# Three changes to the schedule of a fused attention and channel-mix kernel: norm matmuls later and in another PSUM bank, squares in pairs, and one square behind a product

## The chip, the cores and the metric

One core of one Trainium2 chip. The time is that of one execution on the device, in microseconds (us); every figure quoted as a time is the median of several runs. A run's page comes from one profiled execution. The engines are TensorE (PE, with PEld for its weight loads), VectorE (DVE), ScalarE (ACT) and GpSimd (POOL).

Some executions have a mean granted TensorE clock of 0.989 to 0.996 in place of 0.998 to 1.000, and most of these are 1 to 3 us longer (the kernel before: 517.25 at 1.000 and 520.41 at 0.989).

The traces show where the lower clock costs. In profiles at 0.994 to 0.996 the granted clock is 0.83 from 20 to 30 us and 1.00 in the other stretches up to 505 us, and the first matmul of the down projection starts at 52.5 to 53.0 us. So a length measured from that matmul on compares kernels without the clock's disturbance; I call it the length after the head.

## The reference

```python
# attention over channels: q, k, v are [4, 6208, 256]
qn = q / (norm(q, axis=1) + 1e-6);  kn = k / (norm(k, axis=1) + 1e-6)   # norms over the 6208 tokens
s  = kn.transpose(0, 2, 1) @ qn / tau          # 256 x 256 for each batch
a  = softmax(s);   x = v @ a
# channel mix
xk = mu_k * x + (1 - mu_k) * x_prev;   xr likewise with mu_r   # x_prev: the token before
k  = relu(xk @ w_k)                            # 1024 features
out = sigmoid(xr @ w_r) * ((k * k) @ w_v)
```

## The kernel before

The first batch's covariance and softmax make up the first 40 us or so (the head). After that the kernel is a pipeline over blocks of 512 tokens (48 of them, and one of leftovers), with eight steps to a block. In each step TensorE does an up projection for block i+1 (128 features), a part of the down projection for block i, now and then the gate, x of block i+2, and a piece of the covariance of the *next* batch. ScalarE does the relu, the evictions and the squares of q and k; VectorE squares the relu, mixes, and sums the squares. Every instruction's place in the program's order is fixed by hand.

The relu and its square, one 128-feature row at a time:

```python
kr = p2.tile([P, M], BF16, name="kr", tag="kr", bufs=4)
nc.scalar.activation(kr[:, :m], kT_ps[:, :m], AF.Relu, scale=RH)
...
nc.vector.tensor_tensor(st[i, "kk"][:, fh, :m], kr[:, :m], kr[:, :m], op=OP.mult)
```

The norm of one group of 512 tokens: VectorE sums the squares into `t1`, TensorE sums over the partitions by a one-column matmul, ScalarE copies the result out of PSUM. The program places the pool `ps`, into which this kernel's matmuls write, in PSUM; in it the tags `g` (gate) and `xT` (x) own one buffer each, called a bank here, and the norm used the gate's:

```python
n_ps = ps.tile([P, 4], F32, name="n_ps", tag="g")
for i in range(2):
    for h in range(2):
        nc.tensor.matmul(n_ps[:, 2*i+h : 2*i+h+1], t1[:rows, i, h*P:(h+1)*P], ones_b[:rows], ...)
nc.scalar.copy(ssq[b][:, :, g], n_ps)
```

The loop's order, cut to what matters (i is the block, j the step):

```python
if j in (2, 6): gate_act(i, j // 4)            # ScalarE empties the gate's bank
up(i + 1, j)                                   # matmuls, relu
if j > 0: square(i + 1, j - 1)                 # VectorE
...
if j in (0, 1, 4, 5): gate_mm(i, ...)          # fills the gate's bank
down(i, j)
if j in (0, 2): x_half(n, j // 2)              # n = i + 2; fills and empties the bank of x
if j == 4: mix_delta(n)
if j in (5, 6): mix(n, "xk", j - 5)            # VectorE; the next block's up projection needs it
...
elif j in (3, 7) or j in (2, 6) and len(norms) > 1: take_norm()
```

Of the kernel before, what the change touches and what calls it, by code (L numbers as in the profile page):

```python
# [10 lines left out]
F32 = mybir.dt.float32  # L11
BF16 = mybir.dt.bfloat16
AX = mybir.AxisListType.X
AF = mybir.ActivationFunctionType
OP = mybir.AluOpType
# [3 lines left out]
def kernel(  # L19
# [13 lines left out]
    nc = tc.nc  # L33
# [3 lines left out]
    P = 128  # L37
    M = 512
    S = M // P
    assert C == 256 and DF == 1024  # L40
    NB = N // M
# [5 lines left out]
    RH = 0.5 ** 0.5  # L47
# [5 lines left out]
    p2 = ctx.enter_context(tc.tile_pool(name="p2", bufs=3))  # L53
    ps = ctx.enter_context(tc.tile_pool(name="ps", bufs=1, space=bass.MemoryType.PSUM))
# [125 lines left out]
    def broadcast(w, tag, **kw):  # L180
        bc_ps = ps.tile([P, 2, P], F32, name="bc_ps", tag=tag, **kw)
        for h in range(2):
            for u in range(3):
                nc.tensor.matmul(bc_ps[:, h], w[:, u, h:h + 1].to_broadcast([P, P]), ident,
                                 start=h == 0 and u == 0, stop=u == 2, skip_group_check=True)
        return bc_ps.rearrange("p h d -> p (h d)")
# [28 lines left out]
    NBLK = len(blocks)  # L215
# [3 lines left out]
    st = {}  # L219
# [99 lines left out]
    def mix(i, key, dh):  # L319
        mu = mu_k_t if key == "xk" else mu_r_t  # L320
        o = st[i, key]
        if i < LAST:
            c = blocks[i][1] * M
            nc.vector.scalar_tensor_tensor(o[:, dh], st[i, "d"][:, dh], mu[:, dh:dh + 1],  # L324
                                           X[:, dh, c:c + M], op0=OP.mult, op1=OP.add)
        else:
            def r(a):
                return a.rearrange("p (b l) -> p b l", b=B)
            nc.vector.scalar_tensor_tensor(r(o[:, dh, :B * L]), r(st[i, "d"][:, dh, :B * L]), mu[:, dh:dh + 1],
                                           xl[:, dh, :, :L], op0=OP.mult, op1=OP.add)  # L330

    def up(i, fh):
        m = size(i)
        if fh == 0:
            st[i, "kk"] = p2.tile([P, 8, M], BF16, name="kk", tag="kk", bufs=2)
        xk = st[i, "xk"]
        kT_ps = ps.tile([P, M], F32, name="kT_ps", tag="kT", bufs=3)
        for dh in range(2):
            nc.tensor.matmul(kT_ps[:, :m], w_k_sb[:, dh, fh * P:(fh + 1) * P], xk[:, dh, :m],  # L339
                             start=dh == 0, stop=dh == 1)  # L340
        kr = p2.tile([P, M], BF16, name="kr", tag="kr", bufs=4)
        nc.scalar.activation(kr[:, :m], kT_ps[:, :m], AF.Relu, scale=RH)  # L342
        st[i, "kr", fh] = kr

    def square(i, fh):
        m = size(i)
        kr = st.pop((i, "kr", fh))
        nc.vector.tensor_tensor(st[i, "kk"][:, fh, :m], kr[:, :m], kr[:, :m], op=OP.mult)  # L348

    def gate_mm(i, s):  # L350
        if s * P >= size(i):
# [87 lines left out]
    norms = []  # L439

    def take_sum():
        if not sums:
            return
        b, g, w = sums.pop(0)
        rows, n = rows_of(g)
        G = groups[b, g]
        if w == 1:
            nc.vector.tensor_tensor(G["sq", 0], G["sq", 0], G["sq", 1], op=OP.add)  # L448
            return
        t1 = pq.tile([P, 2, C], BF16, name="t1", tag="t1", bufs=4)  # L450
        if w == 2:
            nc.vector.tensor_tensor(t1, G["sq", 0][:, 0], G["sq", 0][:, 1], op=OP.add)
        else:
            nc.vector.tensor_copy(t1[:rows], G["sq", 0][:rows, 0])
        norms.append((b, g, t1))

    def take_norm():
        if not norms:
            return
        b, g, t1 = norms.pop(0)  # L460
        rows, n = rows_of(g)
        n_ps = ps.tile([P, 4], F32, name="n_ps", tag="g")
        for i in range(2):
            for h in range(2):
                nc.tensor.matmul(n_ps[:, 2 * i + h:2 * i + h + 1], t1[:rows, i, h * P:(h + 1) * P], ones_b[:rows],
                                 start=i == 0 and h == 0, stop=True, skip_group_check=True)
        nc.scalar.copy(ssq[b][:, :, g], n_ps)  # L467
        if g == GORD[-1]:
            chain.extend(softmax_pieces(b))
# [8 lines left out]
    def softmax_pieces(b):  # L478
        t_sb, e_sb, sm, mx = soft_tiles()
        hold = {}  # L480

        def a():
            hold["n"] = root(ssq[b], 4)

        def a2():
            hold["r"] = inverse(hold["n"], 4)
            if inv_tau != 1.0:
                nc.vector.tensor_scalar_mul(hold["r"][:, 2:], hold["r"][:, 2:], inv_tau)

        def b1():  # L490
            hold["dq"] = spread(hold["r"])

        def bcast():
            hold["bc"] = pn.tile([P, C], F32, name="rq_bc", bufs=1)
            nc.scalar.copy(hold["bc"], broadcast(hold["dq"], "g"))

        def c():
            nc.vector.tensor_tensor(t_sb, s_sb[b], hold["bc"].unsqueeze(1).to_broadcast([P, 2, C]), op=OP.mult)

        def e():  # L500
            for ih in range(2):
                soft_half(b, ih, t_sb, hold["r"][:, 2:], e_sb, sm, mx)

        def f():
            for ih in range(2):
                soft_scale(b, ih, e_sb, sm)

        return [a, None, a2, b1, None, bcast, None, c, e, f]


# [73 lines left out]
    chain = []  # L584
    lst = {}

    for i in range(-2, NBLK):
        for j in range(8):
            T = i * 8 + j
            if i == LAST - 1 and j == 7:  # L590

                st[LAST, "res"] = pq.tile([P, S, D], F32, name="res", tag="f4", bufs=NF)
                for s in range(2):
                    gate_mm(LAST, s)
                gate_act(LAST, 0)
            if j in (2, 6):
                gate_act(i, j // 4)
            if 0 <= i + 1 < NBLK:
                up(i + 1, j)
            if j == 0 and i >= 0:  # L600
                square(i, 7)
            if j > 0 and 0 <= i + 1 < NBLK:
                square(i + 1, j - 1)
            if j == 5:
                finish(i, 0)
            if j == 1:
                finish(i - 1, 1)
            if i >= 0:
                if j in (0, 1, 4, 5) and i < LAST:
                    gate_mm(i, j // 4 * 2 + j % 4)  # L610
                down(i, j)
            n = i + 2
            if n == 0 and j == 0:
                x_first()
            if 0 < n < LAST:
                if j == 0:
                    x_half(n, 0)
                if j == 2:
                    x_half(n, 1)
            if n < NBLK:  # L620

                d = 4 if n != 1 else 3
                if j == d:
                    mix_delta(n)
                if j in (d + 1, d + 2) and n > 0:
                    mix(n, "xk", j - d - 1)
            if j in (0, 1) and 0 <= i + 1 < NBLK:
                mix(i + 1, "xr", j)
            if j == 7 and 2 <= i + 3 < NPE:
                v_transpose_pe(i + 3, st.pop((i + 3, "v")), 0, S, "s")  # L630
            if j == 1 and NPE <= i + 5 < LAST:
                v_transpose_dma(i + 5)
            if j == 2 and NPE < i + 7 < LAST:
                v_load(i + 7)
            bank_g = False
            if chain and (chain[0] is None or chain[0].__name__ != "bcast" or j in (3, 7)):
                f = chain.pop(0)
                if f is not None:
                    f()
                    bank_g = f.__name__ == "bcast"  # L640
            if bank_g:
                pass
            elif j in (3, 7) or j in (2, 6) and len(norms) > 1:
                take_norm()
            if j in (2, 3, 6, 7) or len(sums) > 2:
                take_sum()
            for u in due.get(T, []):
                b, g, s = units[u]
                at = (b - 1) * (NB + 1) + GORD.index(g)
                more_rows(at + 4)  # L650
                unit(b, g, s)
                if g == GORD[-1] and s == S - 1:
                    evac_s(b)
            if i >= 0 and i // NB < B:
                bl = i // NB
                if i % NB == 2 and j == 1:
                    lst["v"] = left_load(bl)
                if i % NB == 4 and j == 3:
                    lst["t"] = left_transpose(lst["v"])
                if i % NB == 6 and j == 4:  # L660
                    left_x(bl, lst["t"])
# [35 lines left out]
```

## Time and profile before

| | before |
|---|---|
| time, three runs | 517.29 us (517.14 to 517.46) |
| span in the profile | 515.3 us |
| TensorE busy / idle | 492.3 / 23 us, of which 12.5 idle in the first 60 us |
| VectorE busy | 451.3 us |
| ScalarE busy | 435.7 us |

The busy share of an average says little here: read the kernel as a head that is fed by DMA (VectorE's casts wait 11.8 us for the loads of q and 3.6 us for those of k), a long middle (60 to 505 us) in which TensorE is meant never to stop, and a short tail. In the middle, the question is only where TensorE's next matmul started later than the one before it allowed. I call the lateness a hole. (In the waits below, `ssq` is the copied norm, `t` the sum of squares, `v_ps` the down projection and `res` its gated product.) The lines of the profile follow in the prediction.

### The profile page before, as it was taken

Reading aid. Unit: us, or ns where it says so; the run is one execution under the profiler, and the core shown is the slowest. Engines: PE = TensorE matmul, PEld = TensorE weight load, DVE = VectorE, ACT = ScalarE, POOL = GpSimd, SP = SyncE. Lnnn points to the kernel's source line nnn. Section 1 sums busy time; section 2 is a strip of 40 time slices with the busy share of each in tenths; the row PEclk is TensorE's granted clock in tenths of the full one; section 3 lists DMA queues with packets and bytes.
Section 4 is the critical chain, followed back from the end, with each engine's and each line's share of the span. In section 5 each row is a group of like instructions: output and inputs, shape, how many; then the busy total and the mean of one; then the engine's idle time right before and its main releaser. Section 6 shows DMA issues by size and latency. Waiting matters only on the chain. (4 is left out here: it accounts for less than half of the span.)

```text
span 515.3 us, 10233 instructions
## 1 busy us (share of the span) xinstructions
PE 492.3 (96%) x3723; PEld 340.5 (66%) x3786; DVE 451.3 (88%) x899; ACT 435.7 (85%) x832; POOL 104.5 (20%) x145
## 2 busy tenths in 40 slices
PE   4699999999999999999999999999999999999996
PEld 2474676767667677677666767667666666666675
DVE  3468899999999999999999999999989888888884
ACT  5778999999989898899999899899787877777773
POOL 0047523332431231221251132100031000000000
PEclk9999999999999999999999999999999999999999
DMA  8999999999999999599699999962298673332113
GB/s 313 396 321 188 181 201 207 194 201 186 186 186 207 164 170 174 115 173 155 109 185 216 167 178 165 142 129 71 62 170 141 122 126 95 94 88 76 58 67 102
DMA packets 143202, 83.51 MB, mean 162 GB/s; under 512 B 51184, under 2 KB 139824, under 8 KB 143152
## 3 DMA queue, kind: packets, MB, share of 16 engines
q0 software_dynamic: 65808, 33.01, 50.1%
q1 hardware_dynamic: 77184, 49.72, 39.5%
q8 instruction: 29, 0.48, 0.4%
q14 instruction: 21, 0.17, 0.1%
q10 hardware_dynamic: 160, 0.13, 0.1%
HBM read 78.71 MB, written 25.43 MB: 202 GB/s over the span
## 5 line engine op out<-in xcount | busy, mean ns | idle before, releaser
L342 ACT ACTIVATE kr<-kT_ps 128x512 bf16<-128x512 f32 (+1 forms) x392 | 232.5, 595 | 37.0 <-PE kT_ps L339 29.8
L387 PE MATMUL v_ps<-w_v_sb,kk 128*128 128x256 bf16 x1536 | 230.4, 273 | 0.5
L339 PE MATMUL kT_ps<-xk,w_k_sb 128*128 128x512 bf16 (+1 forms) x725 | 218.9, 377 | 3.0 <-DVE xk L324 1.3
L348 DVE TENSOR_TENSOR kk<-kr 128x512 bf16<-128x512 bf16 (+1 forms) x392 | 161.7, 417 | 35.1 <-ACT kr L342 31.4
L387 PEld LDWEIGHTS <-kk 128*128 128x128 bf16 x1536 | 150.2, 98 | 57.6
L430 ACT ACTIVATE sq<-qk 128x512 f32<-128x512 bf16 (+1 forms) x147 | 93.2, 634 | 0.0
L339 PEld LDWEIGHTS <-w_k_sb 128*128 128x128 bf16 x784 | 74.8, 98 | 22.0 <-issue 1.0
L358 PE MATMUL g_ps<-w_r_sb,xr 128*128 128x256 bf16 x388 | 73.9, 272 | 2.5 <-ACT ssq L467 1.3
L260 ACT CAST X<-xT_ps 128x512 bf16<-128x512 f32 x94 | 55.5, 590 | 20.0 <-PE xT_ps L258 19.3
L324 DVE SCALAR_TENSOR_TENSOR xr<-delta,mu_r_t,X 128x512 bf16<-128x512 bf16 x96 | 71.5, 745 | 0.0
L358 PEld LDWEIGHTS <-xr 128*128 128x128 bf16 x388 | 37.8, 98 | 49.0 <-issue 5.9
L324 DVE SCALAR_TENSOR_TENSOR xk<-delta,mu_k_t,X 128x512 bf16<-128x512 bf16 x94 | 70.1, 745 | 0.0
L400 DVE SCALAR_TENSOR_TENSOR res<-res,v_ps 128x512 f32<-128x512 f32 x96 | 65.3, 680 | 0.0
L416 POOL DMA_DIRECT2D qk<-in_q_dram x39 | 28.6, 734 | 164.8 <-ACT sq L430 136.7
L393 ACT ACTIVATE res<-g_ps 128x512 f32<-128x512 f32 x97 | 57.8, 596 | 0.4 <-PE g_ps L358 0.4
L258 PE MATMUL xT_ps<-vT,a_sb 128*128 128x512 bf16 x188 | 55.9, 379 | 0.2 <-ACT X L285 0.2
L426 PE MATMUL s_ps<-qk 128*128 128x256 bf16 (+1 forms) x294 | 56.1, 272 | 0.0
L227 POOL DMA_DIRECT2D v_bf<-in_v_dram x48 | 37.3, 781 | 52.4 <-DMA vT<-v_bf 47.4
L448 DVE TENSOR_TENSOR sq<-sq 128x1024 f32<-128x1024 f32 x36 | 43.9, 1219 | 1.0 <-ACT sq L430 1.0
L426 PEld LDWEIGHTS <-qk 128*128 128x128 bf16 (+1 forms) x294 | 26.6, 97 | 12.1 <-issue 1.3
L313 DVE TENSOR_TENSOR delta<-X 128x1024 bf16<-128x1024 bf16 x48 | 32.9, 686 | 0.1
L416 POOL DMA_DIRECT2D qk<-in_k_dram x39 | 28.9, 741 | 6.8 <-DMA qk<-in_q_dram 2.1
(73 smaller groups left out, 235.1 us busy)
## 6 DMA issues: line engine op xcount, KB each, us to landing
out_dram<-res SPq DMA_DIRECT2D x48, 512.0 KB, 3.3
v_bf<-in_v_dram POOLq DMA_DIRECT2D x48, 256.0 KB, 8.1
qk<-in_q_dram POOLq DMA_DIRECT2D x36, 256.0 KB, 8.5
qk<-in_k_dram POOLq DMA_DIRECT2D x36, 256.0 KB, 9.5
f<-in_q_dram SPq DMA_DIRECT2D x12, 512.0 KB, 8.3
f<-in_k_dram SPq DMA_DIRECT2D x11, 512.0 KB, 9.1
vT<-v_bf SPq DMA_TRANSPOSE x44, 6.7
w_k_sb<-in_moe_w_k_dram POOLq DMA_DIRECT2D x1, 512.0 KB, 6.3
```

Source lines behind the costliest of these rows:

```text
L258: nc.tensor.matmul(xT_ps, a_sb[:, b, ih, dh * P:(dh + 1) * P], vT[:, :, ih, :], start=ih == 0, stop=ih == 1)
L324: nc.vector.scalar_tensor_tensor(o[:, dh], st[i, "d"][:, dh], mu[:, dh:dh + 1], X[:, dh, c:c + M], op0=OP.mult, op1=OP.add)
L339: nc.tensor.matmul(kT_ps[:, :m], w_k_sb[:, dh, fh * P:(fh + 1) * P], xk[:, dh, :m], start=dh == 0, stop=dh == 1)
L342: nc.scalar.activation(kr[:, :m], kT_ps[:, :m], AF.Relu, scale=RH)
L348: nc.vector.tensor_tensor(st[i, "kk"][:, fh, :m], kr[:, :m], kr[:, :m], op=OP.mult)
L358: nc.tensor.matmul(g_ps[:, s % 2], xr[:, dh, s * P:(s + 1) * P], w_r_sb[:, dh, :], start=s % 2 == 0 and dh == 0, stop=dh == 1, skip_group_ ...
L387: nc.tensor.matmul(v_ps[:, s % 2], kk[:, fh, s * P:(s + 1) * P], w_v_sb[:, fh, :], start=s % 2 == 0 and fh == 0, stop=fh == 7, skip_group_ ...
L393: nc.scalar.activation(st[i, "res"][:, 2 * u:2 * u + 2], st.pop((i, "g", u)), AF.Tanh, scale=0.5)
L400: nc.vector.scalar_tensor_tensor(r, r, 1.0, st.pop((i, "v", u)), op0=OP.add, op1=OP.mult)
L416: nc.gpsimd.dma_start(qk[:rows, :n, i], src_rows(t, b, g))
L426: nc.tensor.matmul(cov[b][:, ih, :], qk[:rows, s, 1, ih * P:(ih + 1) * P], qk[:rows, s, 0, :], start=g == GORD[0] and s == 0 and ih == 0, ...
L430: nc.scalar.activation(G["sq", s // 2][:rows, s % 2], qk[:rows, s], AF.Square)
```

## The change

The intent: give TensorE nothing to wait for in the middle. Three things are done. (1) The norm's matmuls (and the spread of r, which happens three times in the run) go to the bank of x, at steps 4 and 6, and not before two steps after their sum. (2) The relu rows are squared two at a time. (3) The square that belongs to step 6 is issued behind the mix of xk.

```diff
-        kr = p2.tile([P, M], BF16, name="kr", tag="kr", bufs=4)
-        nc.scalar.activation(kr[:, :m], kT_ps[:, :m], AF.Relu, scale=RH)
+        if fh % 2 == 0:
+            st[i, "kr", fh // 2] = p2.tile([P, 2, M], BF16, name="kr", tag="kr", bufs=3)
+        nc.scalar.activation(st[i, "kr", fh // 2][:, fh % 2, :m], kT_ps[:, :m], AF.Relu, scale=RH)
 ...
-        nc.vector.tensor_tensor(st[i, "kk"][:, fh, :m], kr[:, :m], kr[:, :m], op=OP.mult)
+        if fh % 2 == 0:
+            return
+        nc.vector.tensor_tensor(st[i, "kk"][:, fh - 1:fh + 1, :m], kr[:, :, :m], kr[:, :, :m], op=OP.mult)
 ...
-        norms.append((b, g, t1))
+        norms.append((b, g, t1, T + 2))          # T counts steps; taken only from then on
 ...
-        n_ps = ps.tile([P, 4], F32, name="n_ps", tag="g")
+        n_ps = ps.tile([P, 4], F32, name="n_ps", tag="xT")
 ...                                              # and the spread of r: "g" -> "xT"
-            if j > 0 and 0 <= i + 1 < NBLK:
+            if j > 0 and j != 6 and 0 <= i + 1 < NBLK:
                 square(i + 1, j - 1)
 ...  (mix of xk at steps 5 and 6)
+            if j == 6 and 0 <= i + 1 < NBLK:
+                square(i + 1, j - 1)
 ...
-            elif j in (3, 7) or j in (2, 6) and len(norms) > 1:
+            if j in (4, 6) and not bank_x or j in (3, 5) and len(norms) > 1:
                 take_norm()
```

More of the change, by code (lines that the diff above doesn't have):

```diff
@@ L340, in up @@
                              start=dh == 0, stop=dh == 1)
-        kr = p2.tile([P, M], BF16, name="kr", tag="kr", bufs=4)
-        nc.scalar.activation(kr[:, :m], kT_ps[:, :m], AF.Relu, scale=RH)
-        st[i, "kr", fh] = kr
+        if fh % 2 == 0:
+            st[i, "kr", fh // 2] = p2.tile([P, 2, M], BF16, name="kr", tag="kr", bufs=3)
+        nc.scalar.activation(st[i, "kr", fh // 2][:, fh % 2, :m], kT_ps[:, :m], AF.Relu, scale=RH)
     def square(i, fh):
         m = size(i)
-        kr = st.pop((i, "kr", fh))
-        nc.vector.tensor_tensor(st[i, "kk"][:, fh, :m], kr[:, :m], kr[:, :m], op=OP.mult)
+        if fh % 2 == 0:
+            return
+        kr = st.pop((i, "kr", fh // 2))
+        nc.vector.tensor_tensor(st[i, "kk"][:, fh - 1:fh + 1, :m], kr[:, :, :m], kr[:, :, :m], op=OP.mult)
     def gate_mm(i, s):
@@ L454, in take_sum @@
             nc.vector.tensor_copy(t1[:rows], G["sq", 0][:rows, 0])
-        norms.append((b, g, t1))
+        norms.append((b, g, t1, T + 2))
     def take_norm():
-        if not norms:
+        if not norms or norms[0][3] > T:
             return
-        b, g, t1 = norms.pop(0)
+        b, g, t1, _ = norms.pop(0)
         rows, n = rows_of(g)
-        n_ps = ps.tile([P, 4], F32, name="n_ps", tag="g")
+        n_ps = ps.tile([P, 4], F32, name="n_ps", tag="xT")
         for i in range(2):
@@ L494, in bcast @@
             hold["bc"] = pn.tile([P, C], F32, name="rq_bc", bufs=1)
-            nc.scalar.copy(hold["bc"], broadcast(hold["dq"], "g"))
+            nc.scalar.copy(hold["bc"], broadcast(hold["dq"], "xT"))
         def c():
@@ L634 @@
                 v_load(i + 7)
-            bank_g = False
-            if chain and (chain[0] is None or chain[0].__name__ != "bcast" or j in (3, 7)):
+            bank_x = i >= 0 and i % NB == 6 and j == 4
+            if chain and (chain[0] is None or chain[0].__name__ != "bcast" or j in (4, 6)):
                 f = chain.pop(0)
@@ L639 @@
                     f()
-                    bank_g = f.__name__ == "bcast"
-            if bank_g:
-                pass
-            elif j in (3, 7) or j in (2, 6) and len(norms) > 1:
+                    bank_x = f.__name__ == "bcast"
+            if j in (4, 6) and not bank_x or j in (3, 5) and len(norms) > 1:
                 take_norm()
```

## The prediction

> **What bounds the kernel now.** I read the busy table of the page first, then the busy time by stretches, then the timeline of one block of 512 tokens, then the waits of TensorE, and last the timeline around each of those waits. The page's first part:
>
> ```profile
> PE 492.3 (96%) x3723; PEld 340.5 (66%) x3786; DVE 451.3 (88%) x899; ACT 435.7 (85%) x832; POOL 104.5 (20%) x145
> ```
>
> TensorE looks full and VectorE is close behind. By stretches of 100 us:
>
> ```profile
> 100.00:200.00 100.00, 98.27 (x738) 68.61 (x750) 96.07 (x187) 91.22 (x188) 28.15 (x38) 1.00 1.21 185
> 200.00:300.00 100.00, 98.79 (x736) 69.19 (x749) 95.86 (x188) 91.08 (x183) 25.04 (x35) 1.00 1.00 162
> 300.00:400.00 100.00, 98.30 (x717) 68.14 (x727) 93.19 (x186) 85.90 (x168) 14.60 (x20) 1.00 0.78 130
> 400.00:500.00 100.00, 99.37 (x686) 67.77 (x696) 84.27 (x176) 77.35 (x139) 1.49 (x2) 1.00 0.39 93
> ```
>
> The columns after the length are busy us of PE, PEld, DVE, ACT and POOL. In the first three stretches DVE is 93 to 96% busy, and in the fourth, when the covariance work (squares, sums, norms) has run out, it drops to 84%. PE gains only about one point from that. So DVE is nearly full, but it does not set the pace. The clock column is 1.00 throughout.
>
> A busy PE may still have holes, because the end of a matmul is modelled, so I looked at starts instead. From one block:
>
> ```profile
> 250.56 0.59 PE L339 MATMUL kT_ps<-xk,w_k_sb 128*128 128x512 bf16 x2
> 251.00 0.38 PE L358 MATMUL g_ps<-w_r_sb,xr 128*128 128x256 bf16 x2
> 251.22 0.71 PE L387 MATMUL v_ps<-w_v_sb,kk 128*128 128x256 bf16 x5
> 251.76 0.38 PE L426 MATMUL s_ps<-qk 128*128 128x256 bf16 x2
> 251.98 0.59 PE L339 MATMUL kT_ps<-xk,w_k_sb 128*128 128x512 bf16 x2
> ```
>
> Two 512-column matmuls occupy 251.00-250.56 = 0.44 us, 0.22 each; five of 256 columns occupy 0.54, 0.11 each; two take 0.22. Each group starts when the one before it has streamed. In a block without a stall nothing remains to be won on PE, whatever the other engines do. The gain of this change can only come from the holes. TensorE's waits over the whole run, apart from the head:
>
> ```profile
> PE g_ps L358 <- ACT ssq L467: 1.3, 4, 0.5
> PE kT_ps L339 <- DVE xk L324: 1.3, 3, 0.6
> PE n_ps L465 <- DVE t L452: 0.5, 1, 0.5
> ```
>
> These are idle times after a modelled end; measured start against due start, each hole is longer. One of the first kind:
>
> ```profile
> 269.20 0.24 PE L465 MATMUL n_ps<-ones_b,t 128*128 128x1 bf16 x4
> 269.52 0.59 PE L339 MATMUL kT_ps<-xk,w_k_sb 128*128 128x512 bf16 x2
> 269.90 0.58 ACT L342 ACTIVATE kr<-kT_ps 128x512 bf16<-128x512 f32 x1
> 270.38 0.16 ACT L467 COPY ssq<-n_ps 128x4 f32<-128x4 f32 x1
> 270.59 0.38 PE L358 MATMUL g_ps<-w_r_sb,xr 128*128 128x256 bf16 x2 [0.47 <-ACT ssq L467]
> ```
>
> The norm's four one-column matmuls wrote the gate's PSUM bank at 269.20. ScalarE was behind with the exponentials of the softmax and copied the result out only at 270.38. The gate's next matmul needs the same bank; due at 269.52+2*0.22 = 269.95, it started at 270.59, a loss of 0.63. One of the second kind:
>
> ```profile
> 389.20 0.39 PE L339 MATMUL kT_ps<-xk,w_k_sb 128*128 128x512 bf16 x1
> 389.40 0.75 DVE L324 SCALAR_TENSOR_TENSOR xk<-delta,mu_k_t,X 128x512 bf16<-128x512 bf16 x1
> 390.20 0.38 PE L339 MATMUL kT_ps<-xk,w_k_sb 128*128 128x512 bf16 x1 [0.60 <-DVE xk L324]
> ```
>
> VectorE had done the softmax's last scaling just before and was behind, so the second half of xk came late: due at 389.42, started at 390.20, a loss of 0.78.
>
> [...]
>
> ```profile
> L348 DVE TENSOR_TENSOR kk<-kr 128x512 bf16<-128x512 bf16 x384 | 159.3, 420 | 32.7 <-ACT kr L342 29.1
> L313 DVE TENSOR_TENSOR delta<-X 128x1024 bf16<-128x1024 bf16 x48 | 32.9, 686 | 0.1
> ```
>
> Same operation class and type: 420 ns for 512 columns, 686 for 1024. The slope is 266/512 = 0.52 ns per column and the fixed part 420-266 = 154 ns.
>
> **The change part by part.**
>
> Squares in pairs: 384 instructions of 420 ns (161.3 us of work) become 192 of 1024 columns, taken at 686 ns (131.7 us). That frees 29.6 us of VectorE, 0.62 per block of some 9.9 us. Its share of busy time in the full stretches should fall from 96 to about 90%. None of it lies on TensorE's path in a normal block. It counts only where VectorE is late. The relu's count and cost on ScalarE do not change. The buffers grow from 4 rows to 3 pairs; a relu now needs the square of three pairs back, which is a slot earlier than before, so no new wait there. The square of the pair (4, 5) also moves behind the mix of xk in its slot, which puts xk, what TensorE waited for, first.
>
> What the pairs cost is latency: rows 6 and 7 of a block are now squared together at the block's start. Row 7's square in the block at 250 ran from 250.10 to 250.53, and its matmul was the fifth of the group at 251.22, so at 251.65. A pair would end some 0.27 later, and row 6 is wanted one matmul earlier (251.54): slack of 0.74 in place of 1.12. It holds in a normal block.
>
> Norms in the bank of x: the same matmuls and the same copies, elsewhere. The gate's bank no longer holds a norm, so its wait goes. The bank of x has one buffer too; x is written at steps 0 and 2 of a block, and the norm now comes at 4 or 6 (3 or 5 if two are queued). The copy has two steps of some 1.2 us before the next x at step 0, and x's own eviction ends before step 4. In the bank of the gate it had one step. The spread of r moves likewise, three times in the run.
>
> Two steps behind the sums: the norm's matmul no longer follows its sum at one step's distance, so the wait for t (once, due 114.77, started 115.45: 0.68) goes.
>
> The sum, from starts against due starts in TensorE's timeline. Gate's bank: 270.59 (0.63), 152.90 (0.63), 79.60 (0.34), 63.64 (0.28), 57.73 (0.31), together 2.19. Late VectorE: 115.45 (0.68), 390.20 (0.78), 371.45 (0.59), 51.48 (0.38), together 2.43. All of it is 4.62 us. I take 80%, 3.7, as removed: the early ones are partly the pipeline filling. The tail loses: the last block's final pair (512 columns, 420 ns) stands where a 256-column square (289) stood, and the last gated product queues behind it on VectorE: +0.15, rounded up from 0.13. New waits in other places, a guess: +0.35. Net -3.2 us: 517.3-3.2 = 514.1.
>
> **The rivals.**
>
> 1. VectorE is the real bound, so its 29.6 us come off the time: 488. For it: 96% busy, and 31 us of VectorE's waits are for relus, a loop through three engines. Against it: matmul starts are at their streaming distance in normal blocks, and at 84% VectorE (400 to 500 us) PE gains one point. I give it about 1%.
>
> 2. The bank of x becomes the new single-buffer wait. x's matmuls would wait for the copy of a norm, or a norm for x's eviction; for it, ScalarE was over 1 us late when the exponentials ran, and x's matmul was already followed closely by its eviction. About 39 norms, a tenth of them hit for 0.5 us: +2, so 516. Against it: two steps of slack.
>
> 3. Pairing starves the down projection: row 6 or 7 late at step 1, 0.2 us in each of 48 blocks, +10 us: 523 or so with the gains counted. Against it: the slack of 0.74, and a VectorE with less to do, not more.
>
> 4. Nothing at all: holes reappear because something else is late (ScalarE at 91%, in the softmax stretch); 517.
>
> **Range and chances.** The ceiling is 4.6 us plus some tenths of holes that I did not count, so 512.4 is the low end. The high end takes half the gain lost again to rivals 2 and 4: 516.4. Two per cent is 10.3 us, more than twice the ceiling, so faster by 2% is all but excluded, and slower by 2% needs rival 3 in full.
>
> **What would show it.** Right: squares of 128x1024, 192 of them, near 686 ns; VectorE near 90% from 100 to 300 us; no wait of g_ps for ssq; the three-line list of TensorE's waits gone or under 1 us; spacing of 0.22 and 0.11 unchanged. Wrong: waits of xT_ps for ssq or of n_ps for X (rival 2), waits of v_ps for kk (rival 3), waits of kT_ps for xk still there (the pairs did not help the late VectorE), or a time under 511, which would mean that starts at streaming distance hid something.

2.19 and 2.43 are 4.62 us of holes, of which 3.7 were taken as removed; less 0.15 for the tail and 0.35 for new waits that is the 3.2. The two rows, 420 and 686 ns, are the trace's own. The relus on ScalarE, said not to change, are 392 of 595 ns on average before and 392 of 598 after. The spacings, too, are in the trace: a matmul of 512 columns (L339) is recorded with 377 ns on average, but from 60 to 505 us the median from its start to the next is 216 ns, and none of 862 is under 214 (256 columns: 109, none of 2151 under 107). That nothing is left to be won at these spacings is my inference from them.

## The result, and the profile after

The result is correct and the first runs gave 512.74 us (512.57 to 513.34) against 517.38 us. Later, more runs gave 512.77 against 517.22: 4.45 us or 0.9% off, where 3.2 was predicted.

A ratio is computed as the mean time of one kernel's fast runs over that of the other's of the same rounds, so it isn't quite the ratio of the medians. It was 0.9898 (0.9859 to 0.9938) in the first call and 0.9928 (0.9909 to 0.9947) in the second; the ratio of the second call's medians is 0.9914. The first has four runs of the kernel before, one of them at 520.59 us, which is enough to move a mean by 0.8 us. I take 4.45 us as the gain; the interval of the second lies wholly under 1.

The busy table of the changed kernel:

```profile
PE 494.5 (97%) x3786; PEld 340.8 (67%) x3786; DVE 439.2 (86%) x703; ACT 431.9 (84%) x832; POOL 106.6 (21%) x145
```

(The count of PE is higher only because the trace before lacks 63 matmul records, 59 of them of the up projection; the two kernels have the same matmuls.) The same stretches from 100 to 300 us:

```profile
100.00:200.00 100.00, 100.00 (x767) 69.97 (x766) 95.39 (x150) 91.46 (x191) 29.99 (x40) 1.00 1.42 178
200.00:300.00 100.00, 100.00 (x756) 69.54 (x755) 94.52 (x149) 89.83 (x183) 26.10 (x34) 1.00 1.27 164
```

TensorE went from 98.3 and 98.8 to 100.0. Part of that is the missing records: the changed kernel's second trace, which lacks 64, shows 99.3 and 99.3. VectorE went only from 96 to 95, where the prediction had 90; that is the first thing to explain. TensorE's waits, all that the profile names, head included:

```profile
PE f_ps L192 <- DVE qb L128: 4.4, 5, 2.6
PE nq_ps L113 <- ACT hsq L130: 3.4, 1, 3.4
PE s_ps L146 <- DVE kb L141: 3.0, 5, 0.9
PE vT_ps L247 <- DMA v_bf<-in_v_dram: 1.0, 1, 1.0
PE xT_ps L258 <- ACT vT L251: 0.2, 1, 0.2
PE v_ps L375 <- DVE res L402: 0.2, 1, 0.2
```

The three waits of the kernel before (g_ps for ssq, kT_ps for xk, n_ps for t) are all gone, and no wait of x's bank took their place. The first three lines are the head, as before. The fourth, a load that landed late, is not in the second profile of the same kernel; this span is 511.4 us, those of the first call's other three executions 510.6 to 510.9.

The situation in which the gate used to wait, ScalarE late after a norm, now looks like this:

```profile
270.63 0.24 PE L467 MATMUL n_ps<-ones_b,t 128*128 128x1 bf16 x4
...
270.78 1.41 DVE L324 SCALAR_TENSOR_TENSOR xk<-delta,mu_k_t,X 128x512 bf16<-128x512 bf16 x2
...
271.51 0.24 ACT L469 COPY ssq<-n_ps 128x4 f32<-128x4 f32 x1
...
271.93 0.69 PE L339 MATMUL kT_ps<-xk,w_k_sb 128*128 128x512 bf16 x2
...
272.10 0.68 DVE L350 TENSOR_TENSOR kk<-kr 128x1024 bf16<-128x1024 bf16 x1
```

The copy still comes 0.88 us after the norm's matmuls, but no matmul needs the bank in that time. And both halves of xk are made in a row, ended by 272.19, before the pair of squares; the two matmuls that need them span 0.69 us, where two without a wait span 0.59. The second of them waited 0.10 us: xk is only just in time.

To count holes I took all matmuls from 57 us to the end, and for each the lateness of its start against the start before it plus that one's streaming time (216 ns for 512 columns, 109 for 256, measured in this trace), less 216 ns for each missing record. This is worked out from the starts in the trace; the sum also holds some 1.2 us of small change that every kernel has (the tail's own wait, 0.4, and the first steps of a norm). Five traces lack records (the kernel before, the changed kernel's second, and runs 2, 3 and 4). Where in them the records are missing isn't certain, so their count is taken from the length after the head, which needs none of them: 1.6 us, the count of the changed kernel's first trace, which is complete, plus what the length exceeds that trace's 459.23 us by.

| kernel | holes, us | time, us |
|---|---|---|
| before | 5.7 | 517.2 |
| changed (profiled twice) | 1.6 and 1.6 | 512.8 |

So 4.1 us of holes went, and 4.45 us of time; the prediction's hole at 51.48 us (0.38) lies before the count and is not in the changed kernel's second trace. Of late xk 0.35 us stays: 0.25 at 368.52 and the 0.10 above, both below what the list of waits names. The experiments repeat this table for every part.

### The profile page after: what moved, and what is told of

Read it like the earlier page. It is cut to its first block, busy times and chain, and to the rows that moved or that the text cites. A ratio compares the mean times of both kernels' runs of the same rounds, so it can differ in the third digit from the quotient of the medians.

```text
span 511.4 us, 9917 instructions
## 1 busy us (share of the span) xinstructions
PE 494.5 (97%) x3786; PEld 340.8 (67%) x3786; DVE 439.2 (86%) x703; ACT 431.9 (84%) x832; POOL 106.6 (21%) x145
## 5 line engine op out<-in xcount | busy, mean ns | idle before, releaser
L339 PE MATMUL kT_ps<-xk,w_k_sb 128*128 128x512 bf16 (+1 forms) x784 | 231.3, 377 | 0.2
L389 PE MATMUL v_ps<-w_v_sb,kk 128*128 128x256 bf16 x1536 | 230.4, 273 | 0.0
L389 PEld LDWEIGHTS <-kk 128*128 128x128 bf16 x1536 | 150.1, 98 | 57.7
L350 DVE TENSOR_TENSOR kk<-kr 128x1024 bf16<-128x1024 bf16 (+1 forms) x196 | 133.2, 681 | 41.3 <-ACT kr L343 39.9
L339 PEld LDWEIGHTS <-w_k_sb 128*128 128x128 bf16 x784 | 74.8, 98 | 21.8 <-issue 1.0
L324 DVE SCALAR_TENSOR_TENSOR xk<-delta,mu_k_t,X 128x512 bf16<-128x512 bf16 x94 | 66.2, 745 | 0.0
L428 PEld LDWEIGHTS <-qk 128*128 128x128 bf16 (+1 forms) x294 | 26.7, 97 | 12.1 <-issue 1.3
```

Source lines behind the costliest of these rows:

```text
L324: nc.vector.scalar_tensor_tensor(o[:, dh], st[i, "d"][:, dh], mu[:, dh:dh + 1], X[:, dh, c:c + M], op0=OP.mult, op1=OP.add)
L339: nc.tensor.matmul(kT_ps[:, :m], w_k_sb[:, dh, fh * P:(fh + 1) * P], xk[:, dh, :m], start=dh == 0, stop=dh == 1)
L350: nc.vector.tensor_tensor(st[i, "kk"][:, fh - 1:fh + 1, :m], kr[:, :, :m], kr[:, :, :m], op=OP.mult)
L389: nc.tensor.matmul(v_ps[:, s % 2], kk[:, fh, s * P:(s + 1) * P], w_v_sb[:, fh, :], start=s % 2 == 0 and fh == 0, stop=fh == 7, skip_group_ ...
L428: nc.tensor.matmul(cov[b][:, ih, :], qk[:rows, s, 1, ih * P:(ih + 1) * P], qk[:rows, s, 0, :], start=g == GORD[0] and s == 0 and ih == 0, ...
```

## The experiments

Ten kernels; runs of the kernel before: 517.22, 517.21 and 517.09 us. All passed the comparison with the reference, number 8 too, whose arithmetic is wrong: the comparison's tolerance lets it through.

**1. The changed kernel again.**

> The changed kernel once more, beside the others and in enough rounds for a narrow interval. If my count of the holes is right (4.6 us of matmul starts later than due, all gone in the changed kernel's trace), the time is 4.4 to 4.9 us under the kernel before, a ratio near 0.991. If the first ratio of 0.9898 was right, the gain is over 5 us and holes were missed.

512.77 us (six runs, 512.66 to 515.42), 4.45 us under the kernel before. The count of holes holds, and the first ratio was too good. After the head both traces are 459.23 us long.

**2. The norms' part alone** (bank of x, steps 4 and 6, delay; squares single and in their old places).

```diff
-        n_ps = ps.tile([P, 4], F32, name="n_ps", tag="g")
+        n_ps = ps.tile([P, 4], F32, name="n_ps", tag="xT")
 ... and the delay and steps of the diff above; nothing of the squares
```

> The norms' and the spread's move into the bank of x alone, two steps behind their sums; squares single as before. By the count of holes it removes those of the gate's bank (2.2 us) and the wait for t (0.7), and leaves those of late xk (1.7): 2.9 us faster, near 514.4. Rival (a VectorE with less work cures all, as ScalarE and VectorE feed each other): next to nothing gained here, under 1 us.

514.94 us, 2.3 us faster, with 3.9 us of holes. The waits of g_ps and n_ps are gone. But the waits of kT_ps for xk, 1.3 us before, grew:

```profile
PE kT_ps L339 <- DVE xk L324: 2.1, 5, 0.6
```

One of the new ones, in the same trace:

```profile
155.07 0.74 DVE L324 SCALAR_TENSOR_TENSOR xk<-delta,mu_k_t,X 128x512 bf16<-128x512 bf16 x1
...
155.73 0.41 DVE L348 TENSOR_TENSOR kk<-kr 128x512 bf16<-128x512 bf16 x1
...
156.06 0.74 DVE L324 SCALAR_TENSOR_TENSOR xk<-delta,mu_k_t,X 128x512 bf16<-128x512 bf16 x1
...
156.86 0.38 PE L339 MATMUL kT_ps<-xk,w_k_sb 128*128 128x512 bf16 x1 [0.57 <-DVE xk L324]
```

Read from top to bottom: VectorE makes the first half of xk, then a square, then the second half, and TensorE waits for it. This is the second batch's softmax (150 us), where the kernel before lost 0.63 us to the gate's bank at 152.90 and then had no wait for xk in the following steps. It looks as if the gate's hole had given VectorE the time to catch up. The order of events fits; I didn't test it by itself. It is more than the same lateness moved on: in this softmax the late xk costs 1.2 us (starts at 146.47 and 156.86), and the gate's hole that went was 0.63.

**3. The squares' part alone** (pairs, and the square of step 6 behind the mix; norms in the gate's bank).

```diff
+        nc.vector.tensor_tensor(st[i, "kk"][:, fh - 1:fh + 1, :m], kr[:, :, :m], kr[:, :, :m], op=OP.mult)
 ... and the move behind the mix; nothing of the norms
```

> The squares in pairs alone, with the square of features 4 and 5 behind the mix of xk; norms and spread in the gate's bank as before. By the count of holes it removes those of late VectorE (2.4 us with the one for t) and leaves those of the gate's bank (2.2): near 514.9, with waits of g_ps for ssq still in the trace. Rival (lighter VectorE cures all): 512.7 as the whole change, no waits of g_ps for ssq.

516.67 us, 0.55 us faster, with 5.7 us of holes, as many as the kernel before: a miss for my count, which had 2.4 fewer, and a plainer one for the rival. Even the 0.55 isn't sure: the interval of its ratio is 0.9978 to 1.0015, and the length after the head is only 0.06 us shorter. The gate's waits are untouched, the wait for t doubled, and most of the wait for xk is gone (0.3 us are left of 1.3):

```profile
PE g_ps L360 <- ACT ssq L469: 1.3, 4, 0.5
PE n_ps L467 <- DVE t L454: 1.0, 2, 0.7
```

A lighter VectorE did not make t punctual: the program still makes t1 in the step before the norm. The two parts alone give 2.28 and 0.55, in sum 2.8, and together 4.45. They aren't additive.

**4. The whole change without the move of one square.**

```diff
-            if j > 0 and j != 6 and 0 <= i + 1 < NBLK:
+            if j > 0 and 0 <= i + 1 < NBLK:
                 square(i + 1, j - 1)
 ...
-            if j == 6 and 0 <= i + 1 < NBLK:
-                square(i + 1, j - 1)
```

> The whole change, but the square of features 4 and 5 stays ahead of the mix of xk in its step. If the shorter work of VectorE cured the late xk, the time stays at 512.7 within 0.3. If it was the order that put xk first, the waits of kT_ps for xk come back: 0.5 to 1.7 us slower.

515.75 us, 3.0 us slower than the whole change, with 4.4 us of holes. Neither expectation had so much. The trace shows why. After the second batch's softmax again:

```profile
153.83 0.68 DVE L350 TENSOR_TENSOR kk<-kr 128x1024 bf16<-128x1024 bf16 x1
...
154.44 0.75 DVE L324 SCALAR_TENSOR_TENSOR xk<-delta,mu_k_t,X 128x512 bf16<-128x512 bf16 x1
...
155.24 0.38 PE L339 MATMUL kT_ps<-xk,w_k_sb 128*128 128x512 bf16 x1 [0.42 <-DVE xk L324]
```

The pair of squares, 0.68 us, stands between the two halves of xk, and TensorE waits 0.42 us for the second. Pairing makes this worse than single squares (run 2, with single squares in the old order, took 514.94 us), so the two lines that move the square are what makes pairing worth while. The softmaxes are not all of it: from 391 to 503 us, where every other kernel here takes 111.93 us for the same blocks, this one takes 112.85, because the second half of xk is some 0.09 us late in nearly every block. These waits are too short for the list, and VectorE is only 81% busy there.

**5. The whole change without the delay.**

```diff
-        norms.append((b, g, t1, T + 2))
+        norms.append((b, g, t1, T))
```

> The whole change without the two steps of delay: a norm may follow its sum at the next step 4 or 6. If the delay was needed, waits of n_ps for t come back, some 0.7 to 0.9 us each and perhaps more than one, so 0.7 to 2 us slower. If the pairs have made VectorE punctual anyway, 512.8 as the whole change.

515.21 us, 2.4 us slower than the whole change, 3.8 us of holes. The delay was needed, as the waits for t are back:

```profile
PE n_ps L467 <- DVE t L454: 1.2, 3, 0.5
```

In the same trace x waits once for its own eviction (0.3 us in the list), and at 372.37 us the down projection waits 0.30 us for a pair of squares, rival 3 in one place. The list of TensorE's waits doesn't name it, since kk is loaded as the weight (`PEld L389 LDWEIGHTS <-kk`, 0.4 us of idle time before them put down to kk) and the wait is that of the load.

**6. The whole change, with VectorE's freed time filled again.**

```diff
         nc.vector.tensor_tensor(st[i, "kk"][:, fh - 1:fh + 1, :m], kr[:, :, :m], kr[:, :, :m], op=OP.mult)
+        nc.vector.tensor_tensor(idle_t, half, half, op=OP.mult)      # 128x4, nobody reads it
```

> The whole change, with one idle VectorE instruction of some 160 ns after each pair of squares, so that VectorE is as busy as before the change, in the new order. If it is the freed 0.62 us per block that removes the late xk, one or two us are given back: 514 to 515, with waits of kT_ps for xk. If it is the order (xk before the square), the time stays within 0.3 of 512.8.

515.13 us, 2.4 us slower than the whole change, 3.6 us of holes. Three of its six runs had a clock of 0.994 or 0.995, which inflates this (they took 515.27 to 517.0, the other three 514.39 to 514.99); the length after the head grew by 1.9 us. The filler took 157 ns on average, and VectorE's busy time is 451.4 us, that of the kernel before to 0.1. So the freed time is worth about half of the gain, given the rest. The waits came back in small pieces:

```profile
PE kT_ps L340 <- DVE xk L325: 0.6, 3, 0.2
PE xT_ps L259 <- ACT X L261: 0.5, 2, 0.3
```

The down projection, too, waited for a pair twice (0.09 us at 105.78 and 0.16 at 116.05).

**7. Norms' part and the new order, with single squares** (steps 5 and 6 both have their square behind the mix).

```diff
-            if j > 0 and 0 <= i + 1 < NBLK:
+            if j > 0 and j not in (5, 6) and 0 <= i + 1 < NBLK:
                 square(i + 1, j - 1)
 ...  (mix of xk)
+            if j in (5, 6) and 0 <= i + 1 < NBLK:
+                square(i + 1, j - 1)
```

> The norms' move, and single squares, of which those of features 4 and 5 stand behind the mix of xk at their steps: the order of the changed kernel without its pairs. If the order is what counts, 512.8 to 513.3, as the whole change. If the freed time of VectorE is needed, 514 or more, with waits of kT_ps for xk (the norms' move alone took 514.9).

513.93 us (five runs), 1.2 us slower than the whole change and 1.0 us faster than the norms' part alone, 2.8 us of holes. It lies between the two expectations: the order without pairs gives a part, the time freed by pairs the rest.

**8. The whole change with 36 of VectorE's wide sums left out** (wrong arithmetic).

```diff
-            nc.vector.tensor_tensor(G["sq", 0], G["sq", 0], G["sq", 1], op=OP.add)
             return
```

> The whole change, and the 36 wide sums of squares (1.22 us each) left out, which gives a wrong result on purpose: 44 us less work on VectorE. If TensorE is the bound from 60 us on and has no holes left, nothing is gained: 512.8 within 0.3. If VectorE still bounds in part, 2 us or more.

512.51 us (four runs), 0.26 us under the whole change, and 1.2 us of holes: the 0.35 us of late xk that the whole change still had are gone. VectorE fell to 81 to 83% from 100 to 400 us and the time did not follow:

```profile
100.00:200.00 100.00, 100.00 (x766) 69.90 (x764) 81.36 (x135) 91.77 (x191) 29.88 (x40) 1.00 1.30 190
```

This closes the rival in which VectorE sets the pace: with 41.6 us less busy time of VectorE (439.2 to 397.6) the length after the head is 0.4 us shorter, and TensorE is at 100.0 in all four stretches from 100 to 500 us.

**9. The whole change with norms and spread in the gate's bank** (steps 3 and 7, but with the delay).

```diff
-        n_ps = ps.tile([P, 4], F32, name="n_ps", tag="xT")
+        n_ps = ps.tile([P, 4], F32, name="n_ps", tag="g")
 ... and steps 3 and 7, and the spread's bank, as before
```

> The whole change, but norms and spread stay in the gate's bank at steps 3 and 7 as before, though two steps or more behind their sums. If the delay alone did what the norms' part gives, 512.8 as the whole change. If the bank counts, waits of g_ps for ssq stay in the trace, 4 of some 0.6 us or less: 514.5 to 516.

516.47 us (five runs), 3.7 us slower than the whole change. Four of the five runs had a clock of 0.995 or 0.996, which inflates this; the single one at 0.999 took 515.11, 2.3 us slower. The trace settles the size: after the head it is 461.95 us long against 459.23, so 2.7 us. It has 4.4 us of holes, and the gate's waits are to the tenth those of the kernel before:

```profile
PE g_ps L360 <- ACT ssq L469: 1.3, 4, 0.5
```

**10. The whole change with single squares in the last block.**

```diff
+        if i == LAST:
+            nc.vector.tensor_tensor(st[i, "kk"][:, fh, :m], kr[:, fh % 2, :m], kr[:, fh % 2, :m], op=OP.mult)
+            return
```

> The whole change with single squares in the last block of 256 leftover tokens alone. If the last pair lengthens the tail by 0.13 us, as the prediction has it, this is 0.1 to 0.2 us faster than the whole change, 512.6 to 512.7, and the end of the trace shows it; the time itself may not tell it from noise. Rival: the last gated product waits for the down projection anyway, and nothing changes.

512.63 us (512.3 to 515.79), which the time alone doesn't tell from 512.77. The chain that ended last does: from the start of the last square to the start of the last gated product it is 2.02 us in the kernel before (509.01 to 511.03), 2.15 in the changed one (505.03 to 507.18) and 2.01 here (505.40 to 507.41). It is the changed kernel with 0.14 us of tail given back.

All together, in order of time (kernels before lie within 0.13 us):

| kernel | holes, us | time, us |
|---|---|---|
| before | 5.7 | 517.2 |
| squares' part alone | 5.7 | 516.67 |
| all, norms in the gate's bank | 4.4 | 516.47 (clock low; 515.11 at 0.999) |
| all, square ahead of the mix | 4.4 | 515.75 |
| all, no delay | 3.8 | 515.21 |
| all, VectorE refilled | 3.6 | 515.13 |
| norms' part alone | 3.9 | 514.94 |
| norms' part and order, single squares | 2.8 | 513.93 |
| whole change | 1.6 and 1.6 | 512.77 |
| all, single squares in the tail | 1.5 | 512.63 |
| all, no wide sums (wrong) | 1.2 | 512.51 |

## Why the prediction was right or wrong

**Right: the place of the gain.** TensorE streams at its spacing and only the holes count: from 60 to 505 us the median from start to start is 216 ns for 512 columns in the traces of both kernels, with none under 214 before and none under 215 after. Time follows holes, each against the whole change: before 4.1 of holes and 4.45 of time; the squares' part 4.1 and 3.9; without the move 2.8 and 3.0; the norms' part 2.3 and 2.2; without the delay 2.2 and 2.4; refilled 2.0 and 2.4; single squares in the new order 1.2 and 1.2. TensorE's busy share, 96% before and 97 and 96% in the two traces of the changed kernel, says nothing of this. The prediction's 99.37 for 400 to 500 us is a matter of missing records, too: the blocks from 391 to 503 us take 111.93 us in the kernel before and in the changed one, so nothing was lost there.

**Right: the three causes.** The gate's bank (run 9), xk behind a late VectorE (runs 2, 4 and 6) and the wait for t (run 5) each come back when their cure is undone.

**Right: the rivals' weights.** VectorE as the bound (rival 1) fell in run 8. Rival 2, x's matmuls behind the copy of a norm or a norm behind x's eviction, is in no trace's list; what showed in that bank was x waiting for its own eviction, 0.5 us in run 6 and 0.3 in run 5. Starving of the down projection (rival 3) is absent from the changed kernel before its last block; it showed, 0.1 to 0.3 us at a time, in runs 5 and 6. It had to be looked for in the waits of the weight loads, for the prediction's sign, a wait of v_ps for kk, didn't appear with it. Rival 4, that nothing is gained because something else is late, fell with the time.

**Wrong in size: "I take 80%, 3.7, as removed" and "New waits in other places, a guess: +0.35".** These two discounts, 0.9 and 0.35, are what lies between 3.2 and 4.45. Measured: 4.1 us of holes went after the head and 0.38 before, 0.35 of late xk stayed, and no new wait appeared but the tail's. My count of the ceiling, 4.62, was good; there was no reason in the profile to think that a fifth of it would stay. The holes I put aside as "the pipeline filling" (57.73, 63.64, 79.60) were waits for the gate's bank like the others, and went with it.

**Wrong in size: "That frees 29.6 us of VectorE, 0.62 per block".** Measured: busy time 451.3 to 439.2, so 12.1 us, 0.25 per block. The durations were right:

```profile
L350 DVE TENSOR_TENSOR kk<-kr 128x1024 bf16<-128x1024 bf16 x192 | 131.5, 686 | 38.6 <-ACT kr L343 37.2
```

What was wrong was to multiply them. Two squares in a row in the kernel before, and two pairs in a row in the changed one:

```profile
390.06 0.76 DVE L348 TENSOR_TENSOR kk<-kr 128x512 bf16<-128x512 bf16 x2
```

```profile
154.95 1.28 DVE L350 TENSOR_TENSOR kk<-kr 128x1024 bf16<-128x1024 bf16 x2
```

Two squares of 0.42 take 0.76, so the second starts 0.34 after the first; two pairs of 0.686 take 1.28, a start-to-start of 0.60. Over all squares that another VectorE instruction followed at once, the median from start to next start is 336 ns (331 squares) and 609 ns for a pair (144 pairs). A pair saves 2 x 336 - 609 = 63 ns and not 2 x 420 - 686 = 154; 192 x 63 ns = 12.1 us, close to what the busy table shows (not every square has a follower at once). The duration that the profile records runs on for some 83 ns after the next instruction has started (medians of the same instructions: 419 against 336 ns, and 691 against 609 for a pair); what a square costs a busy VectorE is the distance to the next start. For TensorE I had minded that, for VectorE not. A larger tile does pay the fixed part once, but that part is smaller than the prediction's 154 ns, which came from the durations: an estimate from the two spacings gives 609 - 336 = 273 ns for 512 columns more, and so 336 - 273 = 63 ns fixed. This is also why VectorE stayed at 95% and not 90.

The two errors met: the VectorE time was overrated two and a half times, and still the little that it freed was worth about 2 us (run 6): the larger holes that came back lie around the softmaxes, at 148 to 155, 266 to 273 and 369 us.

**Missed: the parts are not a sum.** The working gave 2.19 us to the gate's bank and 2.43 to late VectorE and added them. Alone, the norms' part gave 2.28 and the squares' part 0.55; the other 1.6 us need both. And undoing any single one of the five ingredients costs 1.2 to 3.0 us (run 9, the gate's bank, 2.7 by its trace). Experiment 2 shows the pattern: with the gate's holes away, TensorE is there earlier and finds xk not ready. Matched by the matmuls of the down projection, the traces show where the sum fails: around the second and third batch's softmax (137 to 167 us and 245 to 285 us in the kernel before) the norms' part alone loses 0.59 and 0.47 us, the squares' part gains nothing, and the whole change gains 0.58 and 0.53. In the rest of the run after the head the parts do add: 2.9 and 0.1 alone, 3.0 together. Why the late xk there costs more than the gate's hole that it replaces (1.2 us for 0.63) stays open.

**Right, and small:** the tail's +0.15 (0.13 to 0.14 in the chain, run 10).

## What to carry to other kernels

When one engine streams without a break (here TensorE, 216 ns for 512 columns), list its late starts, name what each waited for, and take the sum as the gain; don't discount it by feeling, but don't credit single cures with their own holes either, since here, with the gate's waits gone (1.3 us), those for xk grew from 1.3 to 2.1 us (run 2). Where the next instruction follows at once, cost an instruction by the distance from its start to the next start, not by its duration (here VectorE's squares: 336 and not 420 ns; TensorE's matmuls of 512 columns: 216 and not 377). When an instruction is made longer by merging two, look at what stands behind it in program order: here the merge pays only because the pair goes behind the product that TensorE wants next (3.0 us between the two orders).
